# Attention, a search for experts, and the experts: gate products, row blocks and row buffers in the stretch between

## The chip, the cores and the metric

The kernel runs on one core of a Trainium2 chip. The metric is the device time of one execution in microseconds (us); the kernel before was run three times, and its median is 891.27 us. One more execution was recorded by the hardware profiler, and all rows of a profile come from that one.

## The reference

The program computes attention with a sigmoid in place of the softmax, and sends each of the 3584 tokens to one of eight experts; an expert takes exactly 448 tokens.

```python
# q, k, v: (8, 12, 448, 64) float32
scores = scale * np.matmul(q, k.transpose(0, 1, 3, 2)) - np.log(S)
attn = 1.0 / (1.0 + np.exp(-scores))
x = (attn @ v) transposed to tokens, (3584, 768)

logits = x @ w_gate                     # (3584, 8)
order = np.argsort(-logits.flatten())   # best (token, expert) pairs first
for idx in order:                       # cap = 448
    tok, e = idx // E, idx % E
    if assigned[tok] >= 0 or counts[e] >= cap: continue
    assigned[tok] = e; counts[e] += 1
for e in range(E):
    h = np.maximum(x[assigned == e] @ w1[e], 0)   # 768 -> 1024
    out[assigned == e] = h @ w2[e]                # 1024 -> 768
```

## The kernel before

The order of instructions on each engine is the order in which the Python code issues them; nothing reorders them afterwards. Each engine runs its own list in order, and semaphores make it wait for the others. SyncE (SP) and GpSimd (POOL) issue the transfers.

*Attention.* The loop over i goes through 48 pairs of heads (8 batches of 6). For each it computes the scores, the sigmoid on ACT (tile `at`) and, one pair later, the products with v (`av`, L452): six 128-row products per pair (L461) and, for every second pair, the 64 remaining rows (L467). The result of a pair stands in PSUM (`tp`), transposed, heads down and tokens across. VectorE (DVE) copies it to `xt` (L469) and, for every second pair, adds the remaining rows of the pair before (L471). When a batch is through, `logits` (L476) multiplies `xt` with the gate's weights, 24 small float32 products (L482; the profile counts each twice, since float32 runs in two passes), and adds the result to `LE` (L484). For the last batch the products of its first four pairs are issued ahead of the last `av`, and those of the last two behind it.

*Between.* `rows(b, c)` (L486) makes one block of 112 tokens: six transposes from `xt` to PSUM (`sc`, two banks wide; L490), a copy on ACT to a row buffer `xr` (L492), and a write of 336 KB to the DRAM tensor `xs` (L493, issued by SP). There are 32 such blocks, kept in the list `late`. `R.start` transposes `LE` (L134) to `ML`, from which `keys` and `search` run on DVE: `keys` ends in `r_KT`, TensorE transposes that (L162), and then come 16 steps. In each, DVE counts three times (L173), TensorE sums the counts over partitions in one product (L185, the count product), and DVE makes the next thresholds. Two row blocks are issued with each step, so they stand ahead of its count product in TensorE's list; the first block stands ahead of L134, one behind it, two more ahead of L162. After the search, `pick` names the first expert, SP reads its number (L578) and loads its weights (`wr`, L585), `place` and `lists` make its list of tokens (`r_idx`, L293), and GpSimd gathers the tokens' rows from `xs` (L618). A gather waits until all 32 writes have landed.

*Experts.* For each expert TensorE transposes the gathered rows (L632), ACT and DVE split them in a high and a low part (`xh` L635, `xl` L636), and three products stand for each float32 product (L680 to L684, L715 to L719); ACT and GpSimd or DVE split the weights in the same way (`wh` L596, `wl` L598). The search for the next expert runs beside this.

Of the 8 banks of PSUM, `pa_t` (2) and `pa_s` (3 tiles of 2) serve attention; they are closed after the first row block, and `ps_t` (2), `ps_s` (2 tiles of 2) and `ps_a` (2, the router's) are opened, for the rest of the kernel. A tile in a pool just opened waits for the last reader of the bank it lies in.

Of the kernel before, what the change touches and what calls it, by code (L numbers as in the profile page):

```python
# [7 lines left out]
F32 = mybir.dt.float32  # L8
# [12 lines left out]
TWO23 = float(2 ** 23)  # L21
XR_BUFS = 12
XT_BUFS = 8
XA_BUFS = 4
AT_BUFS = 8
YT_BUFS = 3
LATE_PER_STEP = 2
LATE_KEYS = 2
T_KEYS, T_KE, T_STEP, T_DVE, T_KAP, T_PICK, T_TOT, T_OH, T_BT = 3600, 2100, 2050, 2025, 500, 2600, 600, 3800, 600
SLACK = 150  # L30
CHORE_NS = 1000
# [303 lines left out]
def moe_attention(tc, q, k, v, w_gate, w1, w2, out):  # L335
    nc = tc.nc
    B, H, S, D = q.shape
    DM = H * D
    E, _, F = w1.shape
    CP, NCH, NP, ND, NF = 112, S // 112, H // 2, DM // 128, F // 128  # L340
    G4 = 4
    PSUM = bass.MemoryType.PSUM
    with contextlib.ExitStack() as ctx:
# [4 lines left out]
        actx = contextlib.ExitStack()  # L348
        pctx = contextlib.ExitStack()
        ps_t = pctx.enter_context(tc.tile_pool(name="pa_t", bufs=2, space=PSUM))  # L350
        ps_s = pctx.enter_context(tc.tile_pool(name="pa_s", bufs=3, space=PSUM))
        ld = actx.enter_context(tc.tile_pool(name="ld", bufs=2))
        wk = actx.enter_context(tc.tile_pool(name="wk", bufs=2))
        xa = actx.enter_context(tc.tile_pool(name="xa", bufs=1))

        xs = dr.tile([B * S, DM], F32, name="xs")
        K = Consts()
# [26 lines left out]
        def load(b, g):  # L384


            for i in range(2):
                load_kq(b, 2 * g + i, [(n, j, qn) for n, qn in ((0, nc.sync), (1, nc.gpsimd)) for j in range(2)])
            load_v(b, g, nc.sync)
# [15 lines left out]
        def turn(b, pr):  # L405


            T = KT[b, pr] = wk.tile([128, 2, S], F32, name="kqT", bufs=3)
            N = nat["kq", b, pr]
            parts = [slice(0, 2)] if (b, pr) != (0, 0) else [slice(1, 2), slice(0, 1)]  # L410
            for z in parts:
                nc.vector.transpose(T[:, z].rearrange("p n t -> p (n t)"), N[:, z].rearrange("p n c d -> p (n c d)"))  # L412
            H = wk.tile([128, 2, S], F32R, name="kqH")
            L = wk.tile([128, 2, S], F32R, name="kqL")
            KQ[b, pr] = [x[:, i] for i in range(2) for x in (H, L)]

            def split():
                for z in parts:
                    nc.scalar.activation(H[:, z], T[:, z], AF.Copy)  # L419
                for z in parts:  # L420
                    nc.vector.tensor_tensor(L[:, z], T[:, z], H[:, z].bitcast(F32), OP.subtract)  # L421
            return split
# [3 lines left out]
        def sigmoid(a, p):  # L426
            nc.scalar.activation(a, p[:, :, :S], AF.Sigmoid, bias=bias, scale=1 / math.sqrt(D))  # L427

        def scores(b, pr, c):


            a = AT[b, pr, c] = wk.tile([128, 2, S], F32, name="at", bufs=AT_BUFS)
            p = ps_s.tile([128, 2, 512], F32, name="sc")
            KH, KL, QH, QL = KQ[b, pr]
            for i, (R, M) in enumerate(((KH, QH), (KH, QL), (KL, QH))):
                for j, half in enumerate((LO, HI)):
                    nc.tensor.matmul(p[:, j, :S], R[half, c * 128:(c + 1) * 128], M[half], start=i == 0, stop=i == 2)  # L437
            sigmoid(a, p)

        def rest_scores(b, pr):  # L440


            a = AT[b, pr, 3] = wk.tile([128, 2, S], F32, name="at", bufs=AT_BUFS)
            p = ps_s.tile([128, 2, 512], F32, name="sc")
            for o, T in ((HI, KT[b, pr - 1]), (LO, KT[b, pr])):
                for j, half in enumerate((LO, HI)):
                    nc.tensor.matmul(p[o, j, :S], T[half, 0, S - 64:S], T[half, 1], start=True, stop=True)  # L447
            sigmoid(a, p)

        XT = {}  # L450

        def av(b, pr):  # L452


            if pr == 0:
                XT[b] = xa.tile([128, NP, S], F32, name="xt", bufs=XT_BUFS)
            p = ps_t.tile([128, 512], F32, name="tp")
            g, h0 = (2 * pr) // G4, (2 * pr) % G4
            for c in range(3):
                for j in range(2):  # L460
                    nc.tensor.matmul(p[j * 64:j * 64 + 64, :S], nat["v", b, g][:, h0 + j, c, :],  # L461
                                     AT[b, pr, c][:, j, :], start=(c == 0), stop=(c == 2 and pr % 2 == 0))
            if pr % 2:
                r = ps_t.tile([128, 512], F32, name="tp")
                for j in range(2):
                    for half, o in ((HI, r), (LO, p)):
                        nc.tensor.matmul(o[j * 64:j * 64 + 64, :S], nat["r", b, g][half, j, :],  # L467
                                         AT[b, pr, 3][half, j, :], start=o is r, stop=True)
            nc.vector.tensor_copy(XT[b][:, pr, :], p[:, :S])  # L469
            if pr % 2:  # L470
                nc.vector.tensor_tensor(XT[b][:, pr - 1, :], r[:, :S], XT[b][:, pr - 1, :], OP.add)  # L471

# [3 lines left out]
        def logits(b, prs):  # L476

            s, g = b % 4, b // 4
            p = ps_t.tile([128, 512], F32, name="tp")
            for pr in prs:  # L480
                for c in range(NCH):
                    nc.tensor.matmul(p[32 * c:32 * c + 32, :CP], wgz[:, pr, s, :], XT[b][:, pr, c * CP:(c + 1) * CP],  # L482
                                     start=(pr == prs[0]), stop=(pr == prs[-1]))
            nc.vector.tensor_tensor(LE[:, g], LE[:, g], p[:, :CP], OP.add)  # L484

        def rows(b, c):  # L486
            xr = xa.tile([CP, DM], F32, name="xr", bufs=XA_BUFS)
            p = ps_s.tile([128, 2, 512], F32, name="sc")
            for i in range(NP):
                nc.tensor.transpose(p[:CP, i // 3, (i % 3) * 128:(i % 3) * 128 + 128],  # L490
                                    XT[b][:, i, c * CP:(c + 1) * CP], ident)
            nc.scalar.copy(xr.rearrange("p (h d) -> p h d", h=2), p[:CP, :, :384])  # L492
            nc.sync.dma_start(xs[b * S + c * CP:b * S + (c + 1) * CP], xr)  # L493
# [3 lines left out]
        turn(*pairs[0])()  # L497
        bg = []
        late = [lambda b=b, c=c: rows(b, c) for b in range(B) for c in range(NCH)]
        consts = None  # L500
        for i in range(NPR + 1):
            cur = pairs[i] if i < NPR else None
            nxt = pairs[i + 1] if i + 1 < NPR else None
            old = pairs[i - 1] if i else None
            if cur and cur[1] % 2 == 0:
                nx = i // 2 + 2
                if nx < NPR // 2:
                    load(nx // 3, nx % 3)
            split = turn(*nxt) if nxt else None
            for c in range(3 if cur else 0):  # L510
                scores(*cur, c)
                if c == 0 and split:
                    split()
            if cur is None and bg:
                bg.pop(0)()
            if old:
                av(*old)
            if cur and cur[1] % 2 == 0:
                rest_scores(*nxt)
            if bg:  # L520
                bg.pop(0)()
            if i == 2:
                consts = route_consts(nc, cp, K)
            if consts:
                next(consts, 0)
            if old == (B - 1, NP - 2):
                bg.append(lambda: logits(B - 1, range(NP - 2)))
            if old and old[1] == NP - 1 and old[0] < B - 1:
                bg.append(lambda b=old[0]: logits(b, range(NP)))
        logits(B - 1, [NP - 2, NP - 1])  # L530
        late.pop(0)()

        pctx.close()
        ps_t = ctx.enter_context(tc.tile_pool(name="ps_t", bufs=2, space=PSUM))
        ps_s = ctx.enter_context(tc.tile_pool(name="ps_s", bufs=2, space=PSUM))
        ps_a = ctx.enter_context(tc.tile_pool(name="ps_a", bufs=2, space=PSUM))
        R = Router(tc, K, cp, rw, ps_a)
        R.start(LE)
        late.pop(0)()
        picked, listed = {}, {}  # L540

        def routing():
            for kx in range(E):
                for t in R.phase(kx):
                    if kx not in picked and R.ei is not None:
                        picked[kx] = R.ei
                    yield t
# [6 lines left out]
        while 0 not in picked:  # L554
            next(route)
            steps += 1
            for _ in range(LATE_KEYS if steps == 1 else LATE_PER_STEP):
                if late:
                    late.pop(0)()
        while late:  # L560
            late.pop(0)()
        actx.close()

        wp = ctx.enter_context(tc.tile_pool(name="wp", bufs=4))
        hp = ctx.enter_context(tc.tile_pool(name="hp", bufs=1))
# [250 lines left out]
```

## Time and profile before

| | us |
|---|---|
| three runs | 888.68, 891.27, 891.42 |
| profiled execution | 887.23 |
| its span, first to last instruction | 885.5 |
| attention, to the end of the last product with v | 273.8 |
| between, to the first product of an expert | 61.5 |
| experts | 550.2 |

The profiled execution is 4 us below the median of the three runs. In the rows, times are from the start of the span; a row of the order of time has start, duration, engine, line, operation, output<-inputs, shape and count, and in brackets how long the engine had been idle and who ended that. PEclk is the clock that TensorE was granted, as a share of full speed. The name `sc` stands for any tile two banks wide, and `xr` for row buffers of both kinds (those that `rows` fills and those that a gather fills).

### The profile page before, as it was taken

How to read it: one execution, taken by the hardware profiler on the slowest of the kernel's cores; microseconds unless marked ns; L12 is line 12 of the kernel's file. 1: busy time of each engine (PE TensorE's matmuls, PEld its weight loads, DVE VectorE, ACT ScalarE, POOL GpSimd, SP SyncE). 2: the span in 40 equal slices, each digit the busy share in tenths (PEclk: the TensorE clock that was granted, in tenths of full speed). 3: DMA queues.
4: the chain of work that ended last, by engine and by line, in shares of the span. 5: the costliest groups of instructions: out<-in, count | busy, mean ns of one | idle time of the engine just before them, and what ended most of it. 6: DMA issues, size and time to landing. Idle time of an engine off the chain costs nothing.

```text
span 885.5 us, 16232 instructions
## 1 busy us (share of the span) xinstructions
PE 837.8 (95%) x5507; PEld 639.0 (72%) x5507; DVE 531.4 (60%) x2047; ACT 456.2 (52%) x610; POOL 467.4 (53%) x449
## 2 busy tenths in 40 slices
PE   6999999999998729998999999999999999999996
PEld 3455455455555518987988988988888888889996
DVE  4665555555554778958869779779689521421110
ACT  6777777777774724434424424434434434443431
POOL 9645444444400014846864964873883882752651
PEclk9999999999999969999999999999999999999999
DMA  9876666665603945434443542452552542632511
GB/s 172 168 144 127 132 125 123 131 126 120 138 12 100 299 161 153 136 107 161 136 133 117 146 156 75 157 164 95 153 164 70 178 146 72 228 111 72 192 49 63
DMA packets 203507, 117.57 MB, mean 133 GB/s; under 512 B 143936, under 2 KB 193088, under 8 KB 203424
## 3 DMA queue, kind: packets, MB, share of 16 engines
q1 hardware_dynamic: 190688, 83.03, 36.0%
q0 software_dynamic: 10880, 33.28, 11.9%
q8 instruction: 43, 0.70, 0.3%
q10 hardware_dynamic: 1856, 0.23, 0.2%
q14 instruction: 40, 0.33, 0.1%
HBM read 94.47 MB, written 22.02 MB: 132 GB/s over the span
## 4 chain that ended last, share of the span: by engine, by line
PE 77%; DVE 8%; DMA 5%; issue 4%; POOL 3%; ACT 1%; SPq 1%; POOLq 0%; ACTq 0%; DVEq 0%
PE tp L461 13%; PE sc L437 11%; PE sc L682 8%; PE sc L680 8%; PE sc L684 8%; PE sc L717 6%; PE sc L719 6%; PE sc L715 6%; PE tp L467 2%; DMA xs<-xr 2%; DVE r_junk L173 2%; PE sc L447 2%; PE tp L645 2%; DMA xr<-xs,r_idx 2%; PE tp L632 2%
## 5 line engine op out<-in xcount | busy, mean ns | idle before, releaser
L598 POOL TENSOR_TENSOR wl<-wr,wh 128x768 fp32r<-128x768 f32 (+1 forms) x96 | 205.9, 2155 | 134.6 <-ACT wh L596 126.9
L427 ACT ACTIVATE at<-sc,bias 128x896 f32<-128x896 f32 x168 | 161.0, 1006 | 63.1 <-PE sc L447 38.2
L372 POOL DMA_DIRECT2D nkq<-in_q_dram x188 | 118.6, 646 | 111.5 <-DVE kqT L412 104.7
L719 PE MATMUL sc<-hh,wl 128*128 128x448 f32 (+2 forms) x400 | 151.4, 378 | 0.0
L717 PE MATMUL sc<-hl,wh 128*128 128x448 f32 (+2 forms) x400 | 145.4, 364 | 0.1
L684 PE MATMUL sc<-xh,wl 128*128 128x448 f32 (+2 forms) x396 | 145.4, 367 | 0.0
L682 PE MATMUL sc<-xl,wh 128*128 128x448 f32 (+2 forms) x396 | 144.9, 366 | 0.0
L715 PE MATMUL sc<-hh,wh 128*128 128x448 f32 (+2 forms) x400 | 143.9, 360 | 0.0
L680 PE MATMUL sc<-xh,wh 128*128 128x448 f32 (+2 forms) x396 | 143.8, 363 | 0.0
L173 DVE TENSOR_SCALAR_CACHE_REDUCE r_junk<-r_KE,r_T 128x224 bf16<-128x224 f32 x315 | 123.2, 441 | 0.1
L461 PE MATMUL tp<-at,nv 128*64 128x448 f32 x576 | 118.8, 548 | 0.0
L596 ACT ACTIVATE wh<-wr 128x768 fp32r<-128x768 f32 (+1 forms) x112 | 102.0, 939 | 13.2 <-DMA wr<-in_moe_w_dram 13.1
L692 POOL TENSOR_TENSOR hl<-yt,hh 128x896 fp32r<-128x896 f32 x32 | 68.3, 2136 | 44.5 <-ACT yt L691 41.8
L421 DVE TENSOR_TENSOR kqL<-kqT,kqH 128x896 fp32r<-128x896 f32 (+1 forms) x49 | 52.6, 1073 | 58.3 <-ACT kqH L419 58.2
L688 ACT ACTIVATE hh<-sc 128x896 fp32r<-128x896 f32 x32 | 29.5, 920 | 111.0 <-PE sc L684 111.0
L618 POOL DMA_INDIRECT xr<-xs,r_idx x32 | 32.0, 1002 | 97.5 <-ACT wh L596 86.7
L717 PEld LDWEIGHTS sc<-hl,wh 128*128 128x128 f32 x400 | 75.2, 188 | 7.0 <-issue 1.1
L598 DVE TENSOR_TENSOR wl<-wr,wh 128x768 fp32r<-128x768 f32 (+1 forms) x16 | 25.1, 1571 | 91.7 <-ACT wh L596 91.5
L461 PEld LDWEIGHTS tp<-at,nv 128*64 128x64 f32 x576 | 37.1, 136 | 59.1 <-issue 57.9
L682 PEld LDWEIGHTS sc<-xl,wh 128*128 128x128 f32 x396 | 74.5, 188 | 6.3 <-issue 0.5
L715 PEld LDWEIGHTS sc<-hh,wh 128*128 128x128 f32 x400 | 75.6, 189 | 4.4
L680 PEld LDWEIGHTS sc<-xh,wh 128*128 128x128 f32 x396 | 74.7, 189 | 5.5
(156 smaller groups left out, 1323.7 us busy)
## 6 DMA issues: line engine op xcount, KB each, us to landing
wr<-in_moe_w_dram SPq DMA_DIRECT2D x64, 384.0 KB
wr<-in_moe_w_dram SPq DMA_DIRECT2D x48, 512.0 KB
xs<-xr SPq DMA_DIRECT2D x32, 336.0 KB
nkq<-in_k_dram SPq DMA_DIRECT2D x190, 56.0 KB
nkq<-in_q_dram POOLq DMA_DIRECT2D x188, 56.0 KB, 2.6
nv<-in_v_dram SPq DMA_DIRECT2D x92, 96.0 KB
nr<-in_v_dram SPq DMA_DIRECT2D x46, 32.0 KB
xr<-xs,r_idx POOLq DMA_INDIRECT x32, 4.4
```

The source lines that it names most:

```text
L173: nc.vector.tensor_scalar(junk, KE, T[:, i:i + 1].bitcast(F32), None, OP.is_ge, OP.add, accum_out=cnt[:, i:i + 1])
L372: qn.dma_start(t[o:o + 32, n], rws[x])
L427: nc.scalar.activation(a, p[:, :, :S], AF.Sigmoid, bias=bias, scale=1 / math.sqrt(D))
L461: nc.tensor.matmul(p[j * 64:j * 64 + 64, :S], nat["v", b, g][:, h0 + j, c, :], AT[b, pr, c][:, j, :], start=(c == 0), stop=(c == 2 and pr ...
L596: nc.scalar.activation(hi, raw[u], AF.Copy)
L598: eng.tensor_tensor(lo, raw[u], hi.bitcast(F32), OP.subtract)
L680: nc.tensor.matmul(ph[:, f, lo:hi], wh[:, a, fs], xh[:, dd, lo:hi], start=st, stop=False)
L682: nc.tensor.matmul(ph[:, f, lo:hi], wh[:, a, fs], xl[:, dd, lo:hi], start=False, stop=False)
L684: nc.tensor.matmul(ph[:, f, lo:hi], wl[:, a, fs], xh[:, dd, lo:hi], start=False, stop=en)
L715: nc.tensor.matmul(py[:, d2, :w], wh[:, a, dsl], h1, start=st, stop=False)
L717: nc.tensor.matmul(py[:, d2, :w], wh[:, a, dsl], h2, start=False, stop=False)
L719: nc.tensor.matmul(py[:, d2, :w], wl[:, a, dsl], h1, start=False, stop=(j == 1 and a == 3))
```

## The change

Five edits, all between attention and experts. (1) For the last batch all 24 gate products stand behind the last `av`. (2) The copy of the last pair's result to `xt` is made by ACT, not DVE. (3) No row block stands ahead of `R.start`; three instead of two are issued with the step that ends `keys`. (4) The row blocks have eight row buffers, not four, in a pool of their own (`xo`), which lies where the tiles of attention's loads and scores were. (5) The row blocks have three wide PSUM tiles of their own (`ps_w`), not two; `ps_t` and `ps_s` are opened when the row blocks are through.

```diff
-XA_BUFS = 4
+XO_BUFS = 8
...
-LATE_KEYS = 2
+LATE_KEYS = 3
...
-        ld = actx.enter_context(tc.tile_pool(name="ld", bufs=2))
-        wk = actx.enter_context(tc.tile_pool(name="wk", bufs=2))
         xa = actx.enter_context(tc.tile_pool(name="xa", bufs=1))
+        lctx = contextlib.ExitStack()
+        ld = lctx.enter_context(tc.tile_pool(name="ld", bufs=2))
+        wk = lctx.enter_context(tc.tile_pool(name="wk", bufs=2))
...
-            nc.vector.tensor_copy(XT[b][:, pr, :], p[:, :S])
+            (nc.scalar.copy if (b, pr) == (B - 1, NP - 1) else nc.vector.tensor_copy)(XT[b][:, pr, :], p[:, :S])
...
-            xr = xa.tile([CP, DM], F32, name="xr", bufs=XA_BUFS)
+            xr = xo.tile([CP, DM], F32, name="xr", bufs=XO_BUFS)
...
-            if old == (B - 1, NP - 2):
-                bg.append(lambda: logits(B - 1, range(NP - 2)))
             if old and old[1] == NP - 1 and old[0] < B - 1:
                 bg.append(lambda b=old[0]: logits(b, range(NP)))
-        logits(B - 1, [NP - 2, NP - 1])
-        late.pop(0)()
+        logits(B - 1, range(NP))
 
         pctx.close()
-        ps_t = ctx.enter_context(tc.tile_pool(name="ps_t", bufs=2, space=PSUM))
-        ps_s = ctx.enter_context(tc.tile_pool(name="ps_s", bufs=2, space=PSUM))
+        lctx.close()
         ps_a = ctx.enter_context(tc.tile_pool(name="ps_a", bufs=2, space=PSUM))
+        xo = actx.enter_context(tc.tile_pool(name="xo", bufs=1))
+        ps_s = actx.enter_context(tc.tile_pool(name="ps_w", bufs=3, space=PSUM))
...
         actx.close()
+        ps_t = ctx.enter_context(tc.tile_pool(name="ps_t", bufs=2, space=PSUM))
+        ps_s = ctx.enter_context(tc.tile_pool(name="ps_s", bufs=2, space=PSUM))
```

Lines below L469 have numbers one higher in the changed kernel (L490 becomes L491). TensorE's list from the end of attention to L162, first before (the waits in brackets name the engine or DMA queue whose semaphore is waited for):

```order
L482 MATMUL tp<-xt,wgz 32x112 [waits DVE_49]
L482 MATMUL tp<-xt,wgz 32x112 x15
L461 MATMUL tp<-at,nv 64x448 [waits DMAHW6_49,DVE_49,Activation_49]
...
L482 MATMUL tp<-xt,wgz 32x112 [waits DVE_49,PE_49]
L482 MATMUL tp<-xt,wgz 32x112 x7
L490 MATMUL sc<-ident,xt 112x128 x6
L134 MATMUL rt<-ident,LE 112x128 [waits Activation_49,Pool_49]
L134 MATMUL rt<-ident,LE 112x128 [waits DVE_49]
L490 MATMUL sc<-ident,xt 112x128 x12
L490 MATMUL sc<-ident,xt 112x128 [waits Activation_49]
L490 MATMUL sc<-ident,xt 112x128 x5
L162 MATMUL rt<-ident,r_KT 128x112 [waits DVE_49]
```

The same stretch of TensorE's list in the changed kernel:

```order
L462 MATMUL tp<-at,nv 64x448 [waits DMAHW6_49,DVE_49,Activation_49]
...
L483 MATMUL tp<-xt,wgz 32x112 [waits Activation_49]
L483 MATMUL tp<-xt,wgz 32x112 x15
L483 MATMUL tp<-xt,wgz 32x112 [waits DVE_49]
L483 MATMUL tp<-xt,wgz 32x112 x7
L134 MATMUL rt<-ident,LE 112x128 [waits DVE_49,Pool_49]
L134 MATMUL rt<-ident,LE 112x128
L491 MATMUL sc<-ident,xt 112x128 x18
L491 MATMUL sc<-ident,xt 112x128 [waits Activation_49]
L491 MATMUL sc<-ident,xt 112x128 x5
L162 MATMUL rt<-ident,r_KT 128x112 [waits DVE_49]
```

The 16 gate products of the first four pairs moved behind the products with v and wait for ACT; L134 no longer waits for ACT, and all of the first four row blocks stand behind it, ahead of L162.

ACT's list at the first row blocks' copies, before:

```order
L427 ACTIVATE at<-sc,bias 128x896 [waits PE_49,Activation_49] x5
L492 COPY xr<-sc 112x768 [waits PE_49]
L492 COPY xr<-sc 112x768 [waits PE_49,Activation_49]
L492 COPY xr<-sc 112x768 [waits PE_49] x2
L492 COPY xr<-sc 112x768 [waits DMAHW2_49,PE_49]
L492 COPY xr<-sc 112x768 [waits DMAHW3_49,PE_49,Activation_49]
```

And in the changed kernel:

```order
L428 ACTIVATE at<-sc,bias 128x896 [waits PE_49,Activation_49] x5
L470 COPY xt<-tp 128x448 [waits PE_49]
L493 COPY xr<-sc 112x768 [waits DMASW7_49,DMAHW0_49,DMASW6_49,DMAHW1_49,DMASW5_49,DMAHW2_49,DMASW4_49,DMAHW3_49,DMASW3_49,DMAHW4_49,DMASW2_49,DMAHW5_49,DMASW1_49,DMAHW6_49,DMASW0_49,DMAHW7_49,PE_49,Activation_49]
L493 COPY xr<-sc 112x768 [waits PE_49] x7
L493 COPY xr<-sc 112x768 [waits DMAHW2_49,PE_49,Activation_49]
L493 COPY xr<-sc 112x768 [waits DMAHW3_49,PE_49,Activation_49]
```

The copy of the last pair is new; the first copy that waits for a row's write is the fifth before and the ninth now, and the first of all waits for the transfers whose buffers lay where `xo` now lies. The lists from `pick` on hold the same instructions in the same order on every engine.

## The prediction

> **What bounds the kernel now.** I read the busy times by stage first (span, then windows cut at the last product with v and at the first product of an expert), then TensorE in order of time between the cuts, then who it waits for there. Columns after the window are its length, and the busy us of PE, PEld, DVE, ACT and POOL, then granted clock, DMA share and GB/s.
>
> ```profile
> span 885.5 us, 16232 instructions
> core 0: us, PE busy (x) PEld busy (x) DVE busy (x) ACT busy (x) POOL busy (x), PEclk, DMA share, GB/s
> 0.00:273.80 273.80, 266.56 (x2192) 134.87 (x2192) 148.55 (x201) 199.34 (x219) 128.94 (x223) 1.00 0.61 123
> 273.80:335.30 61.50, 35.09 (x282) 28.09 (x281) 45.80 (x224) 28.57 (x38) 4.18 (x6) 0.81 0.67 217
> 335.30:885.50 550.20, 536.13 (x3037) 475.99 (x3035) 337.06 (x1623) 228.31 (x354) 334.25 (x220) 1.00 0.40 128
> ```
>
> TensorE is busy 97% of both long stages, 57% of the 61.5 us between them. The edits lie in that gap, where the search for the first expert's threshold must end before any weight or row can be fetched. TensorE there, in order of time (start, us, what, idle before it and who ended it):
>
> ```profile
> 269.51 0.97 PE L482 MATMUL tp<-xt,wgz 128*32 128x112 f32 x32
> 270.42 2.48 PE L461 MATMUL tp<-at,nv 128*64 128x448 f32 x12
> 272.82 0.98 PE L467 MATMUL tp<-at,nr 64*64 64x448 f32 x8
> 275.18 0.59 PE L482 MATMUL tp<-xt,wgz 128*32 128x112 f32 x16 [1.37 <-DVE xt L471]
> 275.70 0.87 PE L490 MATMUL sc<-ident,xt 128*112 128x128 f32 x6
> 277.55 0.65 PE L134 MATMUL rt<-ident,LE 128*112 128x128 f32 x2 [0.98 <-ACT xr L492]
> 277.99 3.55 PE L490 MATMUL sc<-ident,xt 128*112 128x128 f32 x18
> 281.87 0.41 PE L162 MATMUL rt<-ident,r_KT 112*128 112x112 f32 x2 [0.34 <-DVE r_KT L153]
> ...
> 284.11 0.16 PE L185 MATMUL rt<-r_cnt,c_G 128*128 128x3 bf16 x1 [0.51 <-DVE r_junk L173]
> 286.65 0.17 PE L185 MATMUL rt<-r_cnt,c_G 128*128 128x3 bf16 x1 [1.02 <-DVE r_junk L173]
> 288.50 0.16 PE L185 MATMUL rt<-r_cnt,c_G 128*128 128x3 bf16 x1 [0.32 <-DVE r_junk L173]
> ...
> 292.20 0.17 PE L185 MATMUL rt<-r_cnt,c_G 128*128 128x3 bf16 x1
> 294.59 0.17 PE L185 MATMUL rt<-r_cnt,c_G 128*128 128x3 bf16 x1
> ...
> 313.13 0.17 PE L185 MATMUL rt<-r_cnt,c_G 128*128 128x3 bf16 x1
> ...
> 316.85 0.16 PE L185 MATMUL rt<-r_cnt,c_G 128*128 128x3 bf16 x1 [1.68 <-DVE r_junk L173]
> ```
>
> L185 is the count product, once in each of the 16 search steps. The first step takes 2.54 us (284.11 to 286.65), the following 1.85 (286.65 to 288.50, and 288.50 to 292.20 holds two); these waited for VectorE alone. From 292.20 to 313.13 nine steps take 20.93, 2.33 each: now TensorE is late, because two row blocks (L490) stand ahead of each count product. The last two steps, with no row block ahead, take 1.86 again. What holds the blocks is the copy out of PSUM, and behind it the write to DRAM (a group of instructions, two pieces of the chain of work around one copy, and a window):
>
> ```profile
> L492 ACT COPY xr<-sc 112x768 f32<-112x768 f32 x32 | 25.4, 800 | 20.1 <-PE sc L490 12.5 <-DMA xs<-xr 6.8 <-ACT xr L492 0.3
> ...
> 285.88 3.84 DMA xs<-xr
> ...
> 289.83 0.81 ACT xr L492
> ...
> 290.65 3.61 DMA xs<-xr
> ...
> 292.00:296.00 4.00, 2.89 (x24) 2.13 (x22) 3.12 (x23) 3.15 (x4) 0.00 (x0) 1.00 0.92 297
> ```
>
> A buffer's round is write 3.84 plus copy 0.81 and handing over, 285.88 to 290.65 = 4.77; four buffers give one row per 1.19 us, which is the pace seen (2.33 for two). The wires are 92% busy at 297 GB/s, so they are not far from their own limit: a row of 344,064 bytes takes 1.16 us at that rate.
>
> **The change, part by part.** *Gate products, ACT copy and the row block ahead of the transpose.* The rows that carry this:
>
> ```profile
> 273.88 0.62 DVE L469 COPY xt<-tp 128x448 f32<-128x448 f32 x1 [3.05 <-PE tp L467]
> 274.42 0.61 DVE L471 TENSOR_TENSOR xt<-tp,xt 128x448 f32<-128x448 f32 x1
> 275.83 0.27 DVE L484 TENSOR_TENSOR LE<-LE,tp 128x112 f32<-128x112 f32 x1 [0.79 <-PE tp L482]
> 278.30 0.42 DVE L135 COPY ML<-rt 112x256 f32<-112x256 f32 x1 [2.20 <-PE rt L134]
> 332.66 0.49 ACT L635 ACTIVATE xh<-tp 128x384 fp32r<-128x384 f32 x1 [5.45 <-PE tp L632]
> ```
>
> The 32 gate products leave the place ahead of the last products with v: 270.42 - 269.51 = 0.91 earlier, so these end at 273.80 - 0.91 = 272.9. Then the copy runs on ACT beside the addition on DVE, where before DVE did one after the other. The ACT copy of 448 columns is estimated at 0.54, between 0.49 for 384 columns and 0.80 for 768; with the 0.08 from product to DVE seen at 273.88, it ends at 273.5, and the addition too. The handing back to TensorE took 0.15 (275.03 to 275.18), so gate products start at about 273.65. All 48 now stand there: 0.91 + 0.59 = 1.5, ending 275.15. Add to LE: 0.06 wait plus 0.27, to 275.5, with nothing left between it and L134: the row block (0.87) and its copy went behind. L134 stood at 277.55, because it waited for that copy; it now starts at 275.5, 2.05 earlier. At the full clock it should also take 0.41 as L162 does, not 0.65; I take 0.2 of that. ML is then ready 2.25 earlier, and everything up to the first count product is a DVE chain: 284.11 becomes 281.85.
>
> What is moved in front of L162 instead: four row blocks stand between the two transposes, where three did. The clock decides whether they are late:
>
> ```profile
> 277.00:278.00 1.00, 0.45 (x3) 0.48 (x4) 0.00 (x0) 0.40 (x1) 0.00 (x0) 0.74 0.00 0
> 278.00:280.00 2.00, 2.00 (x11) 2.00 (x10) 1.60 (x4) 0.43 (x1) 0.00 (x0) 0.50 0.59 180
> 281.00:282.00 1.00, 0.66 (x6) 0.42 (x5) 0.78 (x2) 1.00 (x2) 0.00 (x0) 1.00 0.80 233
> ```
>
> The granted clock fell to 0.50 after TensorE had idled 1.37 + 0.98 = 2.35 us in a stretch of 3.7, and a block then took 3.55 / 3 = 1.18, against 0.87 at most at full clock. After the change the idle pieces there are 0.75 and 0.35, so I take the full clock: four blocks end at 275.9 + 3.5 = 279.4, ahead of r_KT at 281.81 - 2.25 = 279.6. At half clock they end at 275.95 + 4.72 = 280.7, and 1.2 of the 2.25 is left.
> [...]
>
> *Eight row buffers, three wide PSUM tiles.* A copy now waits for the write eight rows back, a block for the copy three back. The 14th count product has row 31 ahead of it; that needs the copy of row 28, that the write of row 20. The first copy ends at about 275.9 + 0.87 + 0.80 = 277.6. At 1.16 per row and 3.84 for a write, write 20 lands at 277.6 + 3.84 + 20 x 1.16 = 304.6; copy 28 ends at 305.4 and block 31 at 306.3. The count product is wanted at 281.85 + 2.54 + 12 x 1.85 = 306.6. So no step waits, by 0.3 us, and by more if the wires' last 8% is used. The search ends 15 intervals after the first product: 281.85 + 2.54 + 14 x 1.85 = 310.3 against 316.85. Of these 6.55, 2.25 is the earlier start and 316.85 - 284.11 - 28.44 = 4.3 the freed steps. The bounds of the second term: 4.3 at best, since a step can't be shorter than its DVE chain. For the other end, the writes' own rows (first and last issue; time to landing):
>
> ```profile
> L493 SPq DMA_DIRECT2D xs<-xr x32: 303/304/353, 277.4 to 314.5; - x32
> ...
> DMA to landing us min/median/max: 3.7/4.4/5.6
> ```
>
> From the first issue to the last landing they took 314.5 + 4.4 - 277.4 = 41.5 us, 1.30 a row with the slow start counted in. At that pace write 20 lands 2.8 later and the 14th product is 2.5 late, which leaves 1.8. I take 4.3, since the pace in the steady stretch was 1.16.
>
> *What follows.* Picks, lists, first weights and gather keep their order. Rows for what could be late:
>
> ```profile
> 322.04 20.73 SPq L585 DMA_DIRECT2D wr<-in_moe_w_dram  x8
> 326.37 0.84 ACT L596 ACTIVATE wh<-wr 128x768 fp32r<-128x768 f32 x1 [0.30 <-DMA wr<-in_moe_w_dram]
> 326.70 0.16 DVE L293 TENSOR_SCALAR r_idx<-rt 128x4 int32<-128x4 f32 x1 [0.32 <-PE rt L291]
> 327.73 1.22 POOL L618 DMA_INDIRECT xr<-xs,r_idx  x1 [86.68 <-ACT wh L596]
> 335.18 0.56 DVE L636 TENSOR_TENSOR xl<-tp,xh 128x384 fp32r<-128x384 f32 x1 [0.85 <-ACT xh L635]
> ```
>
> The last write would land at 277.6 + 3.84 + 31 x 1.16 = 317.4. The gather needs all of them, but its list comes at 326.70 - 6.55 = 320.15: hidden by 2.7. The first weights are issued at 315.5 and meet the last two rows on the same queue: at most 1.9 late, of which DVE's 0.85 of idle at 335.18 covers part, so between 0 and -1.0. I take 0, because a write's 3.84 to its landing is three times its 1.16 on the wires: its data have left the queue well before. The new first ACT copy is queued behind the last sigmoid only; the 16 DMA waits ahead of the first row copy are for loads long landed. In the expert stage every wait is on an event that moves along, so I cost it at nothing.
>
> Sum: 2.25 + 4.3 + 0 = 6.55. The profiled execution took 887.23 (span 885.5), so it would take 880.7. The median of the runs shown is 891.27 (888.68 to 891.42), 4 above the profiled one; against it 884.7.
>
> **Rivals.** *Half clock at the start* (four blocks hold L162): 6.55 - 1.05 = 5.5, so 885.8. For it: the 0.50 above; against: half the idle time. *The writes still set the pace* (1.30 per row with eight in flight): 1.8 in place of 4.3, and 0.5 for late weights, so 3.55, 887.7. For it: 92% busy wires; against: four buffers' round explains the pace by itself. *Given back in the first expert*, where a later wait (weights, splits on POOL) stands at the same time as before: under 2.7, 889 to 891. Against: nothing is loaded before the pick, so nothing there has a time of its own. *Slower*: eight writes in flight hold one another up so that the gather waits for the last. It begins to cost once that lands past 327; to lose 2.7 it must land past 330.4, (330.4 - 281.4) / 31 = 1.58 per row or 218 GB/s, well under anything the window shows.
>
> **Chances.** Forecast 0.56, half clock 0.16, writes' pace 0.13, given back 0.10, slower 0.05. A measurement of this kernel can tell about 0.3%, 2.7 us. The first two and three quarters of the third are faster by more: 0.82; same 0.13; slower 0.05. The range reaches from the full sum taken from the lowest of the runs (888.68 - 6.9, with a little below for a run like the profiled one) = 881.2 to the writes' pace with one us on top, 888.6.
>
> **What the profile would show.** Right: one ACT copy of 448 columns beside the addition, L134 close to 2 us earlier than 277.55 with no row block ahead, a clock of 1.00 up to the row blocks' end, count products 1.85 apart through the whole search, the last at 310 to 311, no copy idle for xs<-xr until the last rows, and an expert stage that lasts its 550 us. Wrong: steps of 2.3 in the second half of the search (writes' pace), blocks of 1.18 ahead of L162 (clock), weights that land more than 4 us after their issue, or a longer expert stage.

## The result, and the profile after

The changed kernel took 882.62 us (median; 881.89 to 884.92), against 891.27 before: a ratio of 0.9914, with a 95% interval of 0.9891 to 0.9936. The profiled execution took 882.62, with a span of 880.8. Faster, as forecast; 2.1 us under the forecast 884.7, and inside its range. By the two profiled executions alone it gained 4.6 us (887.23 to 882.62), by the medians 8.65. That gap is what half of the experiments are about. Two single runs were slow, one of the kernel before (2087.74 us) and one of the experiment "row buffers and PSUM alone" (2855.29); the ratios leave them out, and without them those two medians would be 891.18 and 884.44.

The stages of the changed kernel, cut at the same places as before (length, busy us of PE, PEld, DVE, ACT and POOL, granted clock, DMA share, GB/s). In the changed kernel every line from L355 on, not only those below L469, has a number one higher: its L468 is L467 before.

```profile
span 880.8 us, 16227 instructions
```
```profile
0.00:272.40 272.40, 265.61 (x2160) 134.10 (x2160) 148.24 (x200) 199.37 (x219) 128.57 (x223) 1.00 0.61 123
272.40:328.90 56.50, 32.11 (x313) 27.71 (x313) 45.30 (x223) 27.67 (x39) 4.74 (x6) 0.83 0.72 236
328.90:880.80 551.90, 538.28 (x3037) 477.82 (x3035) 336.89 (x1623) 228.27 (x354) 333.86 (x220) 0.99 0.40 128
```

The stretch between attention and experts fell from 61.5 to 56.5, attention by 1.4 (0.91 of it the gate products of four pairs, which left it; the end of attention varies by some tenths besides), and the expert stage grew by 1.7, which the prediction had named as a sign of being wrong. TensorE between, in order of time:

```profile
271.42 0.98 PE L468 MATMUL tp<-at,nr 64*64 64x448 f32 x8
273.07 1.36 PE L483 MATMUL tp<-xt,wgz 128*32 128x112 f32 x48 [0.68 <-ACT xt L470]
274.92 0.40 PE L134 MATMUL rt<-ident,LE 128*112 128x128 f32 x2 [0.49 <-DVE csum L125]
275.16 2.78 PE L491 MATMUL sc<-ident,xt 128*112 128x128 f32 x24
279.00 0.41 PE L162 MATMUL rt<-ident,r_KT 112*128 112x112 f32 x2 [1.06 <-DVE r_KT L153]
...
281.23 0.16 PE L185 MATMUL rt<-r_cnt,c_G 128*128 128x3 bf16 x1 [0.51 <-DVE r_junk L173]
...
283.77 0.17 PE L185 MATMUL rt<-r_cnt,c_G 128*128 128x3 bf16 x1 [1.02 <-DVE r_junk L173]
...
285.62 0.16 PE L185 MATMUL rt<-r_cnt,c_G 128*128 128x3 bf16 x1 [0.32 <-DVE r_junk L173]
...
305.94 0.17 PE L185 MATMUL rt<-r_cnt,c_G 128*128 128x3 bf16 x1 [0.32 <-DVE r_junk L173]
...
309.63 0.16 PE L185 MATMUL rt<-r_cnt,c_G 128*128 128x3 bf16 x1 [1.69 <-DVE r_junk L173]
```

L134 starts 2.63 earlier (277.55 before) with four row blocks behind it, and L162 waits for DVE, not for the blocks. The steps are 1.85 from the second to the last: 285.62 to 305.94 is eleven of them. The last count product comes at 309.63, 7.22 earlier. The brackets show that each step now waits for DVE, and no longer for TensorE. The copies to the row buffers and the writes (a group, a window, the writes' issues):

```profile
L493 ACT COPY xr<-sc 112x768 f32<-112x768 f32 x32 | 23.9, 802 | 9.6 <-PE sc L491 5.7 <-ACT xr L493 2.8 <-issue 1.1
```
```profile
292.00:296.00 4.00, 3.36 (x31) 3.01 (x30) 3.70 (x25) 3.19 (x5) 0.00 (x0) 1.00 1.00 336
```
```profile
L494 SPq DMA_DIRECT2D xs<-xr x32: 303/535/1664, 276.9 to 308.5; - x32
```

No copy waits for a write any more (6.8 us before), and the wires moved 336 GB/s at a share of 1.00, where four buffers gave 297 at 0.92.

Then a part is lost again. The list, the first gather and the first rows at TensorE, then the first expert's first hidden tile (`hh`):

```profile
319.48 0.16 DVE L293 TENSOR_SCALAR r_idx<-rt 128x4 int32<-128x4 f32 x1 [0.32 <-PE rt L291]
...
320.51 1.79 POOL L619 DMA_INDIRECT xr<-xs,r_idx  x1 [79.80 <-ACT wh L597]
...
325.39 0.87 PE L633 MATMUL tp<-ident,xr 128*128 128x128 f32 x3 [5.96 <-DMA xr<-xs,r_idx]
...
341.46 0.92 ACT L689 ACTIVATE hh<-sc 128x896 fp32r<-128x896 f32 x1 [3.99 <-PE sc L685]
```

The last two in the kernel before:

```profile
331.70 0.87 PE L632 MATMUL tp<-ident,xr 128*128 128x128 f32 x3 [5.05 <-DMA xr<-xs,r_idx]
...
346.24 0.92 ACT L688 ACTIVATE hh<-sc 128x896 fp32r<-128x896 f32 x1 [3.87 <-PE sc L684]
```

The list is 7.22 earlier, but the first gather issues in 1.79 where it took 1.22, and the first rows reach TensorE 6.31 earlier. The first hidden tile is only 4.78 earlier, another 1.53 less, and from there to the end nothing moved by more than 0.2.

### The profile page after: what moved, and what is told of

The parts are those of the page before. It is cut to its first block, busy times and chain, and to the rows that moved or that the text cites. A ratio compares the mean times of both kernels' runs of the same rounds, so it can differ in the third digit from the quotient of the medians.

```text
span 880.8 us, 16227 instructions
## 1 busy us (share of the span) xinstructions
PE 836.0 (95%) x5507; PEld 639.6 (73%) x5507; DVE 530.4 (60%) x2045; ACT 455.3 (52%) x611; POOL 467.2 (53%) x449
## 4 chain that ended last, share of the span: by engine, by line
PE 79%; DVE 10%; issue 4%; POOL 3%; DMA 3%; ACT 0%; ACTq 0%; SPq 0%; POOLq 0%; DVEq 0%
PE tp L462 13%; PE sc L438 11%; PE sc L683 9%; PE sc L681 8%; PE sc L685 8%; PE sc L718 6%; PE sc L720 6%; PE sc L716 6%; DVE r_junk L173 4%; PE tp L468 2%; PE sc L448 2%; PE tp L646 2%; DMA xr<-xs,r_idx 2%; PE tp L633 2%; PE tp L483 1%
```

## Experiments

Times are medians of each kernel's runs, beside runs of the kernel before on the same chip. Since attention ends up to 0.6 us apart in two executions of the same order, the search is compared from the end of the last product with v (L467, L468: start plus duration) to the last count product (L185): 43.05 us before (273.80 to 316.85), 37.23 in the changed kernel (272.40 to 309.63). The 0.91 by which attention ends earlier for want of the moved gate products is not in this column. Each search is from one profile.

| kernel | median us | kernel before, us | ratio (95%) | search, us |
|---|---|---|---|---|
| changed, again | 883.36 | 890.99 | 0.9921 (0.9897 to 0.9945) | 37.23 |
| gate products alone | 888.51 | 890.99 | 0.9984 (0.9968 to 1.0001) | 42.93 |
| row buffers and PSUM alone | 885.37 | 890.99 | 0.9927 (0.9901 to 0.9953) | 37.29 |
| changed, four buffers | 886.00 | 890.99 | 0.9947 (0.9928 to 0.9966) | 41.43 |
| changed, two wide tiles | 883.56 | 890.27 | 0.9921 (0.9903 to 0.9938) | 37.25 |
| changed, DVE copy | 884.59 | 890.27 | 0.9930 (0.9910 to 0.9951) | 37.24 |
| changed, filler once | 883.35 | 890.27 | 0.9921 (0.9902 to 0.9939) | 37.23 |
| before, filler once | 889.91 | 890.27 | 0.9991 (0.9977 to 1.0006) | 44.16 |
| changed, filler twice | 881.10 | 891.42 | 0.9886 (0.9864 to 0.9908) | 37.22 |
| before, filler twice | 887.68 | 891.42 | 0.9960 (0.9947 to 0.9972) | 43.86 |
| changed, early memsets | 883.57 | 891.42 | 0.9923 (0.9904 to 0.9941) | 37.22 |
| changed, filler twice and memsets | 880.51 | 891.42 | 0.9886 (0.9864 to 0.9907) | 37.25 |

**The changed kernel again.** No edit.

> The changed kernel once more, beside the others on one chip. Search: the last of the 16 count products about 7.2 us earlier than in the kernel before (309.6 against 316.85), steps of 1.85 throughout. Whole time: if the expert stage's clock is a matter of phase, the runs spread by some 3 us and the time lies 4.6 to 8 us under the kernel before; if the expert stage always gives 2.6 us back (rival), it lies 4.6 under it every time.

Measured: 882.22 to 885.13, 7.6 under the kernel before by the medians; the last count product at 309.56. The changed kernel's search does the same thing to 0.1 us, the whole time varies by 3. What decides the clock from one execution to the next, phase or something else, isn't shown. In the kernel before the search varies too: up to its end the two filler kernels made from it (below) run the same lists, and there it took 44.16 and 43.86 in place of 43.05. So its first profile was a short one by about 1 us here.

**The gate products alone.** Buffers and PSUM tiles as in the kernel before; the ACT copy, the place of the first row block and the order of the pools stay as in the changed kernel.

```diff
-XO_BUFS = 8
+XO_BUFS = 4
...
-        ps_s = actx.enter_context(tc.tile_pool(name="ps_w", bufs=3, space=PSUM))
+        ps_s = actx.enter_context(tc.tile_pool(name="ps_w", bufs=2, space=PSUM))
```

> The changed kernel with four row buffers and two wide PSUM tiles for the row blocks: the edits at the gate products alone. My theory: L134 starts at about 275 as in the changed kernel, 2.6 us earlier than before, but the first write of a row still goes out at about 277, so the writes' pace (1.16 us per row with four buffers) ends the search almost where it ended before: last count product at 315.8 to 316.5, time 0.4 to 1.0 us under before. Rival (the two gains add): last count product at 314.0, time 2.9 us under before.

TensorE's last products with v, its last count product, and ACT's group of copies:

```profile
271.87 0.98 PE L468 MATMUL tp<-at,nr 64*64 64x448 f32 x8
...
315.78 0.16 PE L185 MATMUL rt<-r_cnt,c_G 128*128 128x3 bf16 x1 [1.68 <-DVE r_junk L173]
```
```profile
L493 ACT COPY xr<-sc 112x768 f32<-112x768 f32 x32 | 25.2, 800 | 15.0 <-DMA xs<-xr 8.2 <-PE sc L491 5.3 <-PE rt L185 1.1
```

L134 came at 275.37, 2.2 earlier than before, yet the last count product just 1.07 earlier, as my theory had it. With four buffers the copies wait for writes again (8.2 us), and the first write goes out at 277.3, when it did before (277.4); so the early start is used up in waiting. How much of it is lost isn't shown: the kernel before differs from itself by as much (searches of 43.05 to 44.16, copies idle for writes 6.8, 8.8 and 6.7 us in its three profiles). The time is 2.5 us under before by the medians, more than the 0.4 to 1.0 expected, and 1.4 by the ratio, with an interval from 2.9 to nothing: not clear.

**Row buffers and PSUM alone.** The reverse: the buffers and pools of the changed kernel, and the gate products, the DVE copy and the first row block where they stood.

```diff
-LATE_KEYS = 3
+LATE_KEYS = 2
...
-            (nc.scalar.copy if (b, pr) == (B - 1, NP - 1) else nc.vector.tensor_copy)(XT[b][:, pr, :], p[:, :S])
+            nc.vector.tensor_copy(XT[b][:, pr, :], p[:, :S])
...
+            if old == (B - 1, NP - 2):
+                bg.append(lambda: logits(B - 1, range(NP - 2)))
...
-        logits(B - 1, range(NP))
+        logits(B - 1, [NP - 2, NP - 1])
...
+        late.pop(0)()
         R = Router(tc, K, cp, rw, ps_a)
```

> Eight row buffers and three wide PSUM tiles, with the gate products, the DVE copy and the row block ahead of L134 as in the kernel before (the router's PSUM pool is opened first, as in the changed kernel, so L134 waits for no copy on ACT). My theory: L134 about 0.9 us earlier than before (276.6), every step 1.85, last count product at 311.3 to 311.8, time 5 us under before. Rival (writes' pace at 1.16 per row holds on whatever the number of buffers): steps of 2.3 in the second half, last count product at 315 to 316, time 1 us under before.

```profile
272.99 0.98 PE L468 MATMUL tp<-at,nr 64*64 64x448 f32 x8
...
276.57 0.38 PE L134 MATMUL rt<-ident,LE 128*112 128x128 f32 x2
...
311.26 0.16 PE L185 MATMUL rt<-r_cnt,c_G 128*128 128x3 bf16 x1 [1.68 <-DVE r_junk L173]
```

All steps 1.85, the end 5.59 earlier, as expected. With a row block ahead, L134 still starts 0.98 earlier than before: `ps_a` is opened first now, in a bank that no copy on ACT has to leave. So about 1 us of the start came from the order in which pools are opened, which the list of five edits doesn't name. Measured from the end of attention this search lasts 37.29, the changed kernel's 37.23. So once the pools are opened in that order, the edits of gate products, copy and row block together bring nothing that can be measured behind the end of attention; their gain is that attention ends earlier without the moved gate products. The ratio, 0.9927, is that of the changed kernel on the same chip (0.9921) within the intervals.

**Four row buffers in the changed kernel** (`XO_BUFS = 4`, three wide tiles kept).

> The changed kernel with four row buffers in place of eight, three wide PSUM tiles kept. My theory: the buffers are what frees the steps; with four the copies wait for writes again, steps of 2.3 in the second half, and the third PSUM tile lets the blocks run just one row further ahead: last count product at 314.5 to 315.5, time 1.5 to 2.5 us under before. Rival (the third PSUM tile frees the steps): 309.6, time as the changed kernel.

```profile
271.41 0.98 PE L468 MATMUL tp<-at,nr 64*64 64x448 f32 x8
...
313.82 0.16 PE L185 MATMUL rt<-r_cnt,c_G 128*128 128x3 bf16 x1 [1.68 <-DVE r_junk L173]
```
```profile
L493 ACT COPY xr<-sc 112x768 f32<-112x768 f32 x32 | 25.2, 800 | 14.2 <-DMA xs<-xr 8.5 <-PE sc L491 5.3
```

4.2 us of search lost again, and the copies wait for writes: it is the buffers. The last count product is 0.7 ahead of what I expected, and the time 5.0 under before, where I expected 1.5 to 2.5. The search is 1.5 shorter than with four buffers and two tiles (42.93), and the medians (886.00 and 888.51) are apart in the same sense: as long as writes set the pace, the third tile seems to be worth over one row. How much isn't shown, since such searches differ by 1.1 in three profiles of one list.

**Two wide PSUM tiles in the changed kernel** (`bufs=2` for `ps_w`, eight row buffers).

> The changed kernel with two wide PSUM tiles for the row blocks in place of three, eight row buffers kept. My theory: ACT's copy (0.75 us) and two blocks fit a step with two tiles, as they did in the first five steps before; the last blocks need a write one row later, which costs at most 0.5 us: last count product at 309.6 to 310.2, time within 0.6 us of the changed kernel. Rival (the third tile carries a part of the gain): steps of over 2 us, last count product past 311, time 1.5 us or more above the changed kernel.

```profile
271.78 0.98 PE L468 MATMUL tp<-at,nr 64*64 64x448 f32 x8
...
310.01 0.16 PE L185 MATMUL rt<-r_cnt,c_G 128*128 128x3 bf16 x1 [1.68 <-DVE r_junk L173]
```

37.25 against 37.23: with eight row buffers the third tile is worth nothing, and the time says the same (0.9921 in both).

**The last pair's copy on DVE again.**

```diff
-            (nc.scalar.copy if (b, pr) == (B - 1, NP - 1) else nc.vector.tensor_copy)(XT[b][:, pr, :], p[:, :S])
+            nc.vector.tensor_copy(XT[b][:, pr, :], p[:, :S])
```

> The changed kernel with the last pair's copy on DVE as before. My theory: the first 32 gate products wait for the copy alone (0.62 on DVE against 0.53 on ACT) and the addition behind it ends while they run, so L134 is 0.1 to 0.2 us later than in the changed kernel and the time the same. Rival (copy and addition one after the other are on the path, as the sum of the prediction had it): L134 0.6 us later, time 0.6 us above.

```profile
271.92 0.98 PE L468 MATMUL tp<-at,nr 64*64 64x448 f32 x8
...
273.65 1.36 PE L483 MATMUL tp<-xt,wgz 128*32 128x112 f32 x48 [0.74 <-DVE xt L470]
...
310.14 0.16 PE L185 MATMUL rt<-r_cnt,c_G 128*128 128x3 bf16 x1 [1.68 <-DVE r_junk L173]
```

The gate products wait 0.74 in place of 0.68; the addition runs until 274.13, under the first of them. The search lasts 37.24. The ACT copy brings nothing; the time differs from the changed kernel's by less than the runs of one kernel do.

**Filler ahead of the first rows.** The same edit in both kernels:

```diff
         for j, n in blocks():
             gather(0, j, n)
+        dm = ps_t.tile([128, 512], F32, name="tp")
+        for _ in range(WARM):      # 32
+            nc.tensor.transpose(dm[:, :128], ident, ident)
```

In the changed kernel:

> The changed kernel with 32 more transposes of the identity on TensorE, behind the list's last product and ahead of the first gathered rows (their result is not used). My theory: TensorE's clock is back at 1.00 when the first rows land, the first expert's products take 0.12 each from the start and not 0.21, the 1.9 us lost in the changed kernel's profile at the first expert come back, and the spread of its runs narrows: time 1.5 to 3 us under the changed kernel. Rival (what was lost there is lost to late weights and rows, not to the clock): first expert's products wait for DMA instead, time the same within 0.5 us.

In the kernel before:

> The kernel before with the same 32 transposes in the same place. My theory: the same 4 to 5 us of half clock at the first expert are in most of its runs too, so it gains 1 to 3 us on the median of the kernel before, and against its profiled execution (887.2), in which the clock came back early, less than 1.5. Rival: no gain at all, since the gathered rows, not the clock, set the first expert's start.

Both fell short: no gain that the runs can tell (883.35 and 889.91). First what the clock does there without filler. The granted clock (third number from the end) at the first products of the first expert, in the kernel before (335 to 337), the changed kernel (328 on), and the changed kernel run again (328 on):

```profile
335.00:337.00 2.00, 1.97 (x15) 1.77 (x14) 1.70 (x4) 0.64 (x2) 0.00 (x0) 0.87 0.77 210
...
328.00:330.00 2.00, 2.00 (x10) 1.79 (x9) 1.20 (x4) 0.98 (x2) 0.00 (x0) 0.50 0.89 239
...
332.00:334.00 2.00, 2.00 (x14) 2.00 (x13) 1.78 (x8) 0.62 (x2) 1.82 (x1) 0.65 0.87 305
```
```profile
328.00:330.00 2.00, 2.00 (x11) 1.79 (x10) 1.73 (x4) 0.61 (x2) 0.00 (x0) 0.53 0.91 276
330.00:332.00 2.00, 2.00 (x19) 2.00 (x19) 1.80 (x12) 1.28 (x3) 0.78 (x1) 1.00 0.86 290
```

Before, the clock came back less than 1 us after the first product (335.31); in the changed kernel's first profile more than 4 us after it, in its second about 2. From the last count product to the first hidden tile that makes 29.39, 31.83 and 29.99 us. With the filler the clock is 1.00 when the first rows come, and the stretch takes 29.61 in the changed kernel: 2.2 of the 31.83 come back, so the 1.5 lost in that profile were the clock's. But that profile was an unlucky one. In the seven others with the changed kernel's pools and no filler the stretch took 29.8 to 31.5, in the three with filler 29.6 to 30.1: once the clock is back, TensorE waits for the second block of rows instead (1.03 us in place of 0.37), so the rival had a part in it. And there is a second such place, at the change from the first to the second expert. The changed kernel, and the same kernel run again:

```profile
400.00:402.00 2.00, 1.01 (x6) 0.62 (x6) 1.22 (x3) 1.15 (x4) 0.00 (x0) 1.00 0.05 14
402.00:404.00 2.00, 1.52 (x9) 1.07 (x10) 1.51 (x5) 1.25 (x4) 0.00 (x0) 1.00 0.00 0
404.00:406.00 2.00, 2.00 (x13) 1.82 (x12) 1.90 (x13) 0.74 (x2) 1.55 (x1) 1.00 0.00 0
```
```profile
398.00:400.00 2.00, 1.01 (x6) 0.62 (x6) 1.10 (x3) 1.15 (x4) 0.00 (x0) 1.00 0.04 12
400.00:402.00 2.00, 1.40 (x8) 0.96 (x9) 1.51 (x4) 1.25 (x4) 0.00 (x0) 0.89 0.00 0
402.00:404.00 2.00, 2.00 (x6) 1.78 (x7) 1.90 (x12) 0.49 (x1) 1.43 (x1) 0.50 0.00 0
```

The same instructions, the same half-empty TensorE (1.01 of 2 us); once the clock stayed at 1.00 and once it fell to 0.50, which cost 1.5 us by the next hidden tile (70.45 us from the first expert's first hidden tile to the second's, and 71.99). With the filler once, it fell there for longer and cost more (2.9 us in the changed kernel, 2.4 in the one before), so that in these profiles what came back at the first place went at the second. The filler needn't be the reason: the kernels with the DVE copy and with the row buffers alone lost about 2.5 there without it. The changed kernel with the filler once:

```profile
402.00:404.00 2.00, 1.94 (x8) 1.58 (x7) 1.32 (x6) 1.39 (x3) 0.02 (x1) 0.50 0.00 0
404.00:406.00 2.00, 2.00 (x7) 1.66 (x6) 1.86 (x13) 0.00 (x0) 1.83 (x2) 0.50 0.00 0
```

**Filler at both places.** As above, and between the row transposes of the second expert:

```diff
+        spun = []
...
+            def spin(j):
+                if j == 1:
+                    spun.append(ps_s.tile([128, 2, 512], F32, name="sc"))
+                for _ in range((0, 12, 6, 5)[j]):
+                    nc.tensor.transpose(spun[0][:, 0, :128], ident, ident)
...
-                                       lambda j=j, n=n, hf=hf: xturn(kx + 1, j, n, hf, False)))
+                                       lambda j=j, n=n, hf=hf: (spin(j) if (kx, hf) == (0, 0) else None,
+                                                                xturn(kx + 1, j, n, hf, False))))
```

In the changed kernel:

> The changed kernel with filler transposes of the identity at both places where TensorE starves: 32 ahead of the first gathered rows, and 12, 6 and 5 between the row transposes at the change from the first to the second expert (their results are not used). My theory: with TensorE kept busy the clock drops at neither place; the second expert's first hidden tile comes as far ahead of the kernel before as the first one does (6.5 us), and the spread of the runs narrows: time 881 to 882, 1.5 to 2 us under the changed kernel. Rival (the clock at the change of expert has nothing to do with the time): no change against the changed kernel.

In the kernel before:

> The kernel before with the same filler at both places. My theory: with the clock's luck taken out on both sides, the profiled executions of this kernel and of the changed kernel with the same filler differ by what the search shows, less the longer first gather: 6 to 7 us, where the profiled executions of the kernels themselves differed by 4.6. Time 887.5 to 889. Rival (the expert stage of the changed kernel is longer by itself, from the other place of its tiles): a difference of 4 to 5 us again.

The windows at both places and the first hidden tile, the changed kernel with filler, then the kernel before with filler:

```profile
326.00:328.00 2.00, 0.84 (x9) 0.62 (x8) 1.22 (x3) 0.87 (x2) 0.59 (x3) 1.00 0.97 332
...
340.17 0.92 ACT L689 ACTIVATE hh<-sc 128x896 fp32r<-128x896 f32 x1 [3.86 <-PE sc L685]
...
402.00:404.00 2.00, 1.93 (x11) 1.54 (x11) 1.51 (x8) 1.40 (x3) 0.34 (x1) 1.00 0.00 0
```
```profile
332.00:334.00 2.00, 0.85 (x6) 0.64 (x6) 1.90 (x5) 0.87 (x2) 1.05 (x4) 1.00 0.89 292
...
346.67 0.92 ACT L688 ACTIVATE hh<-sc 128x896 fp32r<-128x896 f32 x1 [3.86 <-PE sc L684]
...
408.00:410.00 2.00, 1.77 (x11) 1.19 (x10) 1.51 (x5) 1.25 (x4) 0.00 (x0) 1.00 0.00 0
```

The clock holds at both. The changed kernel comes to 881.10 (880.25 to 881.92, a spread of 1.7 in four runs in place of 3), the one before to 887.68, 3.7 under itself without filler (and a spread of 2.7 in place of 4.8). Between the two: 6.6 by the medians, 7.0 by the profiled executions (888.92 and 881.92). That is the change without the clock's luck at these two places, and it follows from the stretch between: in this pair the last count product comes 7.33 earlier (310.05 and 317.38), and the first hidden tile, behind the longer first gather, 6.50. The rival, an expert stage longer by itself, would have shown 4 to 5. One piece of luck stays in: the search of the kernel before, 43.86 here.

**Early memsets for the gather's tiles.**

```diff
-            t = xg[kx, j] = xp.tile([128, DM], F32, name="xr", bufs=XR_BUFS)
+            if (kx, j) not in xg:
+                xg[kx, j] = xp.tile([128, DM], F32, name="xr", bufs=XR_BUFS)
+            t = xg[kx, j]
...
+        for j, n in blocks():
+            xg[0, j] = xp.tile([128, DM], F32, name="xr", bufs=XR_BUFS)
+            nc.gpsimd.memset(xg[0, j][:1, :1], 0.0)
         while 0 not in listed:
```

> The changed kernel with four one-element memsets by GpSimd, into the tiles of the first gather, ahead of the first expert's list: the waits for whoever used that memory stand there and no longer at the gather. My theory: the 18 waits of the first gather are why it issues in 1.79 us and not 1.22; it issues in 1.22 or less, the first rows land 0.5 us earlier after the list, time 0.5 us under the changed kernel, within what a run can tell. Rival (the first indirect transfer takes longer for another reason, not the waits): 1.79 again.

GpSimd's first gather in that kernel:

```profile
320.55 1.78 POOL L621 DMA_INDIRECT xr<-xs,r_idx  x1 [7.07 <-DVE wl L599]
```

The memsets, which carry the waits now, ran at 313.3, 7 us ahead of the gather, and it still took 1.78. My theory fell; what makes it longer stays open. It took 1.78 or 1.79 in the changed kernel and in three kernels made from it (filler at both places, early memsets, both), and 1.22 in the kernel before without filler and with filler at both places; the mean of the four gathers was 1158 ns in the changed kernel and 1158 to 1160 in five others with its pools, two of them with four row buffers.

**All three.** The two edits above together.

> All three together on the changed kernel: filler at both places and the early memsets. Theory: the gains add to 2 to 2.5 us, time 880.5 to 882, below both kernels. Rival (filler ahead of the first rows delays them once these come earlier): as the filler alone or slower.

880.51 (880.21 to 881.55), ratio 0.9886: with the filler alone 0.9886 as well. Both beat the changed kernel's 882.6 to 883.6; between them nothing can be told. The gain is the filler's.

## Why the prediction was right, and where it was not

*Start.* Forecast: last product with v at 272.9, ACT copy 0.54, gate products 1.5, L134 at 275.5 and taking 0.41, clock at 1.00. Measured: 272.40, 0.53, 1.36, 274.92, 0.40, 1.00. From the end of the products to L134 it was 2.52 against 2.6; the rest is attention's end. The reasons given for it were wrong in part: the ACT copy beside the addition saves nothing, since the addition ends under the gate products with either engine (37.24 with the DVE copy). And the wait for the first row's copy, 0.98, is gone by the order of the pools alone, with the row block where it was (37.29).

*Half clock ahead of L162.* It didn't come: the four blocks took 2.78, 0.70 each, and L162 waited for DVE. Seven more profiles with this start show no half clock there either: the four blocks took 2.78, or 1.47 and 1.57 with two wide tiles. TensorE's idle pieces ahead of them were 0.68 and 0.49, where the kernel before had 1.37 and 0.98. In the kernel before it is a matter of luck: in its profile with filler at both places, whose filler comes later, the same list had the same pauses, yet L134 took 0.40, where it took 0.65 in the two other profiles; so the pauses alone don't decide it.

*Steps.* 4.3 forecast, 4.34 measured, with no step held; the wires carried a row in 1.02 us (336 GB/s), less than the 1.16 that I counted with. The writes' pace, the second rival, was out. That the figure agrees so closely is luck: it is the excess over free steps in one profile of the kernel before, and in its two others the steps took 33.85 and 33.80 us from first to last count product, 5.4 over the changed kernel's 28.40. That without the buffers the start brings just 1.07 of its 2.2 by the end of the search was not in the prediction; its two terms stand side by side there.

*What follows, costed at nothing.* This is the step that failed, though the forecast time came near. "Every wait is on an event that moves along" holds for the waits, but the granted clock doesn't move along. The first gather took 0.9 of the 7.22 until its rows were there, and the clock at the first expert 1.5, so the profiled executions differ by 4.6 and not 6.55. That looks like the rival "given back in the first expert", but nothing there stood at an old time, and the filler took the clock's part out again. Why the first gather takes longer stays open.

*The forecast against the median* rested on the profiled execution of before being like its other runs. It wasn't: its search was a short one, the clock came back early at the first expert and didn't fall at the second. With the clock's luck gone at both places on both sides the change is worth 6.6 to 7.0. That is close to the 6.55 of the sum, but by two errors that nearly cancel: the last count product came 7.2 to 7.3 earlier, and the first gather gave 0.8 to 0.9 back. Against the medians as they fell it is 7.6 to 8.65, so 884.7 was 2 us high for a reason that is not in the change, and that it lies so near is luck in part.

## What to carry to other kernels

Where a ring of buffers feeds writes, divide its round (copy plus time to landing) by the number of buffers and set that beside the time that the wires need: at 4.77 / 4 = 1.19 against 1.02, buffers were missing, not bandwidth. An earlier start of a chain pays in full only if nothing that starts at the same time as before sets its end (2.2 us of start brought 1.07 with the gate products alone), so try both halves of such a change alone. And before a few tenths of a per cent are read from one profile, look for places where TensorE is half empty: two profiles of the changed kernel differ by 1.8 us at one such place and by 1.5 at the other, in opposite senses, and a little filler in both versions gives the comparison without that.

## What the hardware showed that I had not expected

The clock fell to 0.50 at the second expert though TensorE was busy for about half of the time (0.85, 1.01 and 1.40 us in the three windows of 2 us from 396 to 402) and had its longest pause there in this row (the changed kernel run again, order of time; 1.50 us, the others 0.85 and 0.71):

```profile
397.12 0.85 PE L633 MATMUL tp<-ident,xr 128*128 128x128 f32 x6 [1.50 <-DMA xr<-xs,r_idx]
```

It fell in some executions and not in others of the same program (1.00 and 0.50 in the two windows above). What decides it isn't shown. With that idle time filled the clock stayed at 1.00 at this place in all three profiles in which it was done.
